# Down products that read the second weight's columns in pairs 64 apart, in an attention and gated-layer kernel

## Chip, cores and metric

The kernel runs on one core of one Trainium2 chip. The metric is the device time of one execution in microseconds (us); the median over several runs is what counts. Engines: TensorE (PE, with its weight loads as PEld), VectorE (DVE), ScalarE (ACT), GpSimd (POOL) and SyncE (SP, which issues the DMAs here).

## The reference

Two stages. The first is a linear attention with a decaying state, for 4 batches, 8 heads, 768 tokens and heads of 48:

```python
for t in range(S):
    state = alpha[:, :, t, :, None] * state + einsum('bhd,bhe->bhde', k[:, :, t], v[:, :, t])
    y[:, :, t] = einsum('bhd,bhde->bhe', q[:, :, t], state)
```

The second takes the 3072 tokens of 384 numbers through a gated layer of 2048:

```python
h = x @ w_in                      # (3072, 384) @ (384, 2048)
sp = where(h > 20, h, log1p(exp(minimum(h, 20))))
g = h * tanh(sp)
return (g @ w_out).astype(float32)   # (3072, 2048) @ (2048, 384)
```

The weights arrive as 64-bit numbers; the result is float32.

## The kernel before

Tokens are handled in 24 chunks of 128 rows (two batches of 64 tokens each, C = 128). Attention is done chunk by chunk; its result x stands in SBUF as `xs`, transposed and split into an upper and a lower float32r part. Each weight is likewise split into two float32r parts, `wi` (w_in) and `wo` (w_out, `[128, 2, 16, 384]`), as it arrives: VectorE takes the 64-bit words apart (lines 435 to 445) and makes most of the remainders (line 464), ScalarE rounds (line 450). Later the weights are loaded again and checked on ScalarE (lines 502 and 505).

The gated layer is cut into units: one of the 16 slices f of the 2048 inner columns, for two chunks (the first segments) or four (the others). The list SEGMENTS says in which order. A unit does:

- the up products, line 819: 9 matmuls (3 blocks of rows by 3 pairs of upper and lower parts). The stationary tile is a block of `wi`, the moving one is `xs` through `by_token`, which takes a chunk's 128 columns as pairs: column t of the first batch, then column t of the second, 64 words further on. For four chunks that is 512 columns;
- the gate: five ScalarE operations (lines 828 to 846) and two of VectorE (840, 849), which leave `g`, again in two parts, columns in the order of the pairs;
- the down products, line 877: for each chunk 3 matmuls, the stationary tile a 128x128 block of `g`, the moving one `wo[:, z, f]`, 384 columns in their order. They add up over f in one PSUM bank per chunk.

Four banks o0 to o3 hold these sums. When a segment leaves its chunks before the last f, the sums are stashed in SBUF by ScalarE (`stash`, line 897). At the last f a stashed part is added by VectorE (`join`, line 904), and `result` (line 911) is a ScalarE copy with a running sum for a final test, from PSUM where nothing was stashed, from SBUF after a join. Then SP stores the rows (line 918).

The order of the work is made by a planner in the kernel's own code, class Plan. Each step is a task with an engine, a cost and a lateness (table COST, in us) and a key; keys are moved by hand-kept numbers (SHIFT), the banks of early attention chunks are listed (EARLY_BANKS). `order` walks through time and takes, over all engines, the task that can begin first, keys breaking ties; buffers go round in the order of keys. Where TensorE would be idle before 130 planned us, it puts in filling matmuls (line 928) on bf16 zeros-and-ones data of 384 columns, whose result nobody reads. The order found is written into the program; on the chip each engine keeps to it and waits by semaphores.

The lines that matter:

```python
by_token = lambda t: t.rearrange("p n (x t) -> p n t x", x=2)
# line 819
p[:, :N], wi[:, z, s, fs], by_token(x[:, s, :, a]), start=m == 0,
# line 877
o.tile[:, :DM], g.tile[:, a, j * C : (j + 1) * C], wo[:, z, f],
```

Of the kernel before, what the change touches and what calls it, by code (L numbers as in the profile page):

```python
# [14 lines left out]
AF = mybir.ActivationFunctionType  # L15
# [14 lines left out]
P = 128  # L30
# [37 lines left out]
FILL_FROM, FILL_UNTIL = 2.0, 130.0  # L68
FILL_MARGIN = 0.1
EARLY_BANKS = {  # L70
    0: "att o0 o1 att h".split(),
    1: "att att h o2 h".split(),
    2: "o2 o1 att o0 att".split(),
    3: "att o0 o3 att att".split(),
    4: "att att o2".split(),
    5: "att o2 att".split(),
    10: "o1 o2 o3".split(),
    11: "att o1 att".split(),
    12: "o1 o2 o0".split(),
    13: "att o3 att".split(),  # L80
    14: "att o2 o0".split(),
    15: "h att att".split(),
    16: "o0 o1 att".split(),
    17: "o1 att o3".split(),
    18: "o0 o1 att".split(),
    19: "att att h".split(),
    20: "att o2 att".split(),
    21: "att o0 h".split(),
    23: "att h att".split(),
}  # L90
SHIFT = {
    "chunk": {
# [4 lines left out]
    },  # L97
    "unit": {
# [16 lines left out]
    },  # L115
    "weight": {
        0: -6.4516, 1: -18.694, 2: -0.0718, 3: -5.3782, 4: 0.59055, 5: -3.1028, 6: 0.22915,
        7: 3.6276, 8: -0.93908, 9: 4.1863, 10: -1.3406, 11: -0.89088, 12: 0.60959, 13: 2.7395,
        14: 2.9243, 15: 3.4437,
    },  # L120
    "weight check": {
        0: 3.4663, 1: 0.17532, 3: 5.129, 4: 4.2064, 5: 0.81532, 6: 4.6598, 7: 4.2295, 8: -5.8016,
        9: 1.9332, 10: -0.19251, 11: -6.9069, 12: -0.12023, 13: -4.9148, 14: 4.4556, 15: 14.881,
    },
}
X_PE = 4
# [25 lines left out]
class Plan:  # L152
# [131 lines left out]


WINDOW = 10**6
SAME = 0.2
QUEUE = 8
DMA_FIRST, DMA_LAST = 1.67, 0.3
SLACK, SLACK_FROM = (0.5, 0.3), 12.0  # L290

COST = {
    "load part": (0.47, 0.9), "load qk": (0.47, 1.75), "load q": (0.47, 3.2),
    "load v": (0.47, 0.6), "load w": (0.45, 2.35), "move": (0.625, 0.15), "store": (0.62, 0.9),
    "cold fill": (0.321, 0.36), "fill": (0.1635, 0.2), "off": (0.21, 0.37), "w off": (0.965, 1.09), "lead": (0.27, 0.37), "bits": (0.47, 0.585), "w hi": (0.415, 0.53), "w lo": (0.95, 1.08),
    "w check": (0.89, 1.1),
    "scan": (1.152, 1.27), "inverse": (0.113, 0.21), "mult k": (0.562, 0.745), "mult": (0.602, 0.725), "half mult": (0.32, 0.46), "check": (0.2, 0.34),
    "state": (0.272, 0.4), "state0": (0.21, 0.35), "decay": (0.469, 0.605), "mask": (0.335, 0.49),
    "scores0": (0.7, 0.83), "scores": (0.92, 1.06), "y0": (1.15, 1.27), "y": (1.37, 1.5),
    "y last": (0.935, 1.05), "turn": (0.35, 0.68),  # L300
    "turned": (0.415, 0.57), "update": (0.65, 0.87),
    "x hi": (0.265, 0.415), "x lo": (0.333, 0.45),
    "down": (0.5235, 0.79), "stash": (0.36, 0.5), "join": (0.468, 0.59), "result": (0.485, 0.61),
}
for _n in range(1, 5):
    _c = 128 * _n
    COST["up", _n] = (9 * (0.428e-3 * _c + 0.01), 9 * (0.428e-3 * _c + 0.01) + 0.205)
    COST["exp", _n] = (0.142 + 0.836e-3 * _c, 0.29 + 0.836e-3 * _c)
    COST["act", _n] = (0.094 + 0.836e-3 * _c, 0.237 + 0.836e-3 * _c)
    COST["ln", _n] = (0.186 + 0.836e-3 * _c, 0.327 + 0.836e-3 * _c)  # L310
    COST["dve", _n] = (0.069 + 1.045e-3 * _c, 0.21 + 1.045e-3 * _c)
# [4 lines left out]
def fast_path(ctx, tc, qka, v, w, out, good):  # L316
# [28 lines left out]
    minus1 = const.tile([P, 1], F32, name="minus1")  # L345
    nc.vector.memset(minus1, -1.0)
    by_pair = lambda t: t.rearrange("p (j t) -> p j t", j=NPAIR)
    by_token = lambda t: t.rearrange("p n (x t) -> p n t x", x=2)
    by_half = lambda t: t.rearrange("p (j x t) -> p j x t", j=NPAIR, x=2)
    by_seg = lambda t: t.rearrange("p (n t) -> p n t", n=NSEG)  # L350
# [28 lines left out]
    def new(buffer, shape, name, pool=None, dtype=F32):  # L379
        buffer.tile = (pool or sb).tile(  # L380
            shape, dtype, tag=buffer.tag, name=name, bufs=plan.slots[buffer.tag]
        )
        return buffer.tile
# [421 lines left out]
    def unit(c0, nt, f, at, ends):  # L805
# [61 lines left out]
        for j in range(nt):  # L867
            n = c0 + j
            begins = n not in sums
            if begins:  # L870
                sums[n] = bank(f"o{BANK[n]}")
            o, end = sums[n], ends(n)

            def down(o=o, j=j, n=n, begins=begins, end=end):
                within(o)
                for m, (a, z) in enumerate(((0, 0), (0, 1), (1, 0))):
                    made = nc.tensor.matmul(  # L877
                        o.tile[:, :DM], g.tile[:, a, j * C : (j + 1) * C], wo[:, z, f],
                        start=begins and m == 0, stop=end and m == 2,
                    )  # L880
                if f == NFF - 2 and j == 0:
                    late[mybir.EngineType.PE] = made

            t_down = add(
                "PE", *COST["down"], key + LAG + 0.001 * j, down, [t_lo, *ready_w[f, 1]], [g, o],
                behind=downs.get(n, []),
            )
            downs[n] = [t_down]
            if not end:
                continue  # L890
            del sums[n]
            k = key + LAG + 0.1
            if f < NFF - 1:
                part[n] = plan.buffer("osb")

                def stash(o=o, n=n):
                    nc.scalar.copy(new(part[n], [P, DM], f"part{n}"), o.tile[:, :DM])

                kept[n] = add("ACT", *COST["stash"], k, stash, [t_down], [o, part[n]])
                continue  # L900
            done, from_part = [t_down], n in kept
            if from_part:
                def join(o=o, n=n):
                    nc.vector.tensor_tensor(part[n].tile, o.tile[:, :DM], part[n].tile, ALU.add)

                done = [add("DVE", *COST["join"], k, join, [t_down, kept[n]], [o, part[n]])]
            osb = part[n] if from_part else plan.buffer("osb")

            def result(o=o, n=n, osb=osb, from_part=from_part):
                to = osb.tile if from_part else new(osb, [P, DM], f"osb{n}")  # L910
                nc.scalar.activation(
                    to, to if from_part else o.tile[:, :DM], AF.Copy, accum_out=ochk[:, n : n + 1]
                )

            def store(n=n, osb=osb):
                b, c = chunks[n]
                to = out[2 * b * S : 2 * (b + 1) * S, :].rearrange("(x s) d -> s x d", x=2)
                nc.sync.dma_start(to[c * HALF : (c + 1) * HALF], osb.tile)

            written = add("ACT", *COST["result"], k, result, done, [osb] if from_part else [o, osb])  # L920
            add("SP", *COST["store"], k, store, [written], [osb])

# [274 lines left out]
```

## Time and profile before

| what | value |
|---|---|
| median of 3 runs | 500.67 us (500.38 to 500.82) |
| the profiled execution | 500.14 us |
| its span, first to last instruction | 498.3 us |
| mean granted TensorE clock | 0.997 |
| TensorE matmuls busy | 481.0 us, 5229 of them |
| ScalarE busy | 396.8 us |
| VectorE busy | 326.0 us |
| moved by DMA | 56.82 MB |

All times are of one profiled execution, in us from the first instruction, unless ns is written. Matmuls overlap: one starts while the one before is still ending, so the mean time of one is longer than the distance between two, and a busy TensorE need not be at its peak. "Idle before" is an engine's idle time in front of the instructions of a row, with what ended it. The chain is the work that ended last, followed back from the end; a piece of it on TensorE holds a run of matmuls, with their count. A line such as L877 is a line of the kernel before.

### The profile page before, as it was taken

Reading aid. Unit: us, or ns where it says so; the run is one execution under the profiler, and the core shown is the slowest. Engines: PE = TensorE matmul, PEld = TensorE weight load, DVE = VectorE, ACT = ScalarE, POOL = GpSimd, SP = SyncE. Lnnn points to the kernel's source line nnn. Section 1 sums busy time; section 2 is a strip of 40 time slices with the busy share of each in tenths; the row PEclk is TensorE's granted clock in tenths of the full one; section 3 lists DMA queues with packets and bytes.
Section 4 is the critical chain, followed back from the end, with each engine's and each line's share of the span. In section 5 each row is a group of like instructions: output and inputs, shape, how many; then the busy total and the mean of one; then the engine's idle time right before and its main releaser. Section 6 shows DMA issues by size and latency. Waiting matters only on the chain.

```text
span 498.3 us, 12735 instructions
## 1 busy us (share of the span) xinstructions
PE 481.0 (97%) x5229; PEld 431.9 (87%) x5229; DVE 326.0 (65%) x632; ACT 396.8 (80%) x902; POOL 2.4 (0%) x12
## 2 busy tenths in 40 slices
PE   7999999999999999999999999999999999999994
PEld 4578989989888989879988899999889899999993
DVE  8999999999994777788623489633383433333231
ACT  2677988998989997989998866866966868877872
POOL 1000000000000000000000000000000000000000
PEclk9999999999999999999999999999999999999998
DMA  8686435433334735675330254000130000100001
GB/s 304 213 289 218 155 126 195 149 111 143 128 128 135 270 116 197 215 265 180 144 122 0 75 172 142 32 1 1 64 99 17 8 11 0 53 11 2 0 1 68
DMA packets 20079, 56.82 MB, mean 114 GB/s; under 512 B 4016, under 2 KB 12464, under 8 KB 20016
## 3 DMA queue, kind: packets, MB, share of 16 engines
q1 hardware_dynamic: 20016, 55.96, 32.2%
q8 instruction: 42, 0.69, 0.5%
q14 instruction: 21, 0.17, 0.1%
HBM read 48.87 MB, written 4.72 MB: 108 GB/s over the span
## 4 chain that ended last, share of the span: by engine, by line
PE 55%; DVE 20%; ACT 19%; issue 4%; DMA 1%; ACTq 0%; DVEq 0%
PE bank L877 24%; PE bank L819 21%; PE bank L608 4%; ACT t L834 3%; DVE t L840 3%; ACT t L828 3%; DVE g L849 2%; DVE w_lead L445 2%; DVE w_lead L440 2%; ACT t L831 2%; ACT wc L502 2%; ACT g L846 2%; ACT wc L505 2%; ACT t L837 2%; DVE rest L562 2%
## 5 line engine op out<-in xcount | busy, mean ns | idle before, releaser
L877 PE MATMUL bank<-wo,g 128*128 128x384 f32 x1152 | 218.4, 339 | 1.1 <-DVE xs L691 1.1
L819 PE MATMUL bank<-xs,wi 128*128 128x512 f32 (+1 forms) x954 | 206.1, 364 | 2.8 <-DVE t L840 2.4
L877 PEld LDWEIGHTS bank<-wo,g 128*128 128x128 f32 x1152 | 202.0, 188 | 6.3 <-issue 1.7
L819 PEld LDWEIGHTS bank<-xs,wi 128*128 128x128 f32 x954 | 165.1, 189 | 25.7 <-DVE t L840 6.9
L840 DVE SCALAR_TENSOR_TENSOR t<-t,bank 128x512 f32<-128x512 f32 (+1 forms) x106 | 67.7, 638 | 96.7 <-ACT t L837 96.6
L849 DVE SCALAR_TENSOR_TENSOR g<-t,g 128x512 fp32r<-128x512 f32 (+1 forms) x106 | 67.2, 643 | 40.6 <-ACT g L846 40.4
L846 ACT ACTIVATE g<-t 128x512 fp32r<-128x512 f32 (+1 forms) x106 | 61.0, 584 | 29.4 <-PE bank L877 18.1
L828 ACT ACTIVATE t<-bank 128x512 f32<-128x512 f32 (+1 forms) x106 | 58.1, 549 | 29.7 <-PE bank L819 25.6
L834 ACT ACTIVATE t<-t,fifth 128x512 f32<-128x512 f32 (+1 forms) x106 | 71.9, 679 | 1.7
L837 ACT ACTIVATE t<-t 128x512 f32<-128x512 f32 (+1 forms) x106 | 62.2, 588 | 1.6
L831 ACT ACTIVATE t<-t 128x512 f32<-128x512 f32 (+1 forms) x106 | 62.1, 587 | 1.5
L562 DVE TENSOR_TENSOR_SCAN rest<-qka,behind 112x520 f32<-112x520 f32 x24 | 29.8, 1242 | 0.4 <-DMA qka<-in_qka_dram 0.3
L575 DVE TENSOR_TENSOR_SCAN qka<-qka,ahead 112x520 f32<-112x520 f32 x24 | 29.7, 1236 | 0.0
L686 ACT ACTIVATE xs<-bank 112x256 fp32r<-112x256 f32 x48 | 16.0, 382 | 10.2 <-PE bank L672 6.4
L642 DVE COPY_PREDICATED probs<-causal,bank 128x256 f32<-128x256 uint32 x48 | 18.7, 440 | 3.7 <-PE bank L631 3.7
L608 PE MATMUL bank<-qka,state 48*48 48x64 f32 (+1 forms) x704 | 20.2, 221 | 0.7 <-ACT t L831 0.4
L828 ACT ACTIVATION_READ_ACCUMULATOR t<-bank 128x1 f32 x106 | 20.6, 195 | 0.0
L792 DVE TENSOR_TENSOR state<-bank,state 112x192 f32<-112x192 f32 x40 | 13.2, 353 | 9.7 <-PE bank L672 5.7
L608 PEld LDWEIGHTS bank<-qka,state 48*48 48x48 f32 (+1 forms) x704 | 15.7, 127 | 4.3 <-issue 2.1
L445 DVE SCALAR_TENSOR_TENSOR w_lead<-ws,w_lead 128x384 int32<-128x384 int32 x32 | 19.3, 605 | 0.0
L440 DVE SCALAR_TENSOR_TENSOR w_lead<-ws,w_lead 128x384 int32<-128x384 int32 x32 | 19.0, 608 | 0.0
L608 PEld LDWEIGHTS bank<-probs,v 64*48 64x48 f32 (+1 forms) x768 | 13.4, 127 | 6.3 <-issue 2.1
(76 smaller groups left out, 343.0 us busy)
## 6 DMA issues: line engine op xcount, KB each, us to landing
qka<-in_qka_dram SPq DMA_DIRECT2D x22, 772.5 KB, 5.4
ws<-in_wp_dram SPq DMA_DIRECT2D x16, 768.0 KB, 4.1
wc<-in_wp_dram SPq DMA_DIRECT2D x16, 768.0 KB, 5.1
v<-in_vp_dram SPq DMA_DIRECT2D x24, 192.0 KB, 3.0
out_dram<-osb SPq DMA_DIRECT2D x16, 192.0 KB, 2.3
xs<-xs SPq DMA_DIRECT2D x144, 16.0 KB, 3.2
out_dram<-part SPq DMA_DIRECT2D x8, 192.0 KB, 2.3
qka<-in_qka_dram SPq DMA_DIRECT2D x2, 260.5 KB, 3.6
```

What stands on the lines that cost most here:

```text
L562: nc.vector.tensor_tensor_scan(t[:, :0:-1], alpha()[:, :0:-1], behind[:, ::-1], 0.0, ALU.mult, ALU.max)
L575: nc.vector.tensor_tensor_scan(a, a, ahead, 0.0, ALU.mult, ALU.max)
L608: return nc.tensor.matmul(summed(x)[HALF * side : HALF * side + wide, j], weights(wide), moving, start=start, stop=stop, skip_group_check= ...
L819: nc.tensor.matmul(p[:, :N], wi[:, z, s, fs], by_token(x[:, s, :, a]), start=m == 0, stop=m == len(passes) - 1,)
L828: nc.scalar.activation(wide(t), wide(h), AF.Exp, accum_out=uchk[:, at : at + 1])
L831: nc.scalar.activation(wide(t), wide(t), AF.Square, bias=1.0)
L834: nc.scalar.activation(wide(t), wide(t), AF.Ln, bias=fifth, scale=0.2)
L837: nc.scalar.activation(wide(t), wide(t), AF.Exp, scale=-1.0)
L840: nc.vector.scalar_tensor_tensor(wide(t), wide(t), 2.5, wide(h), ALU.subtract, ALU.mult)
L846: nc.scalar.activation(g.tile[:, 0, :N], wide(t), AF.Copy, scale=-0.4)
L849: late[mybir.EngineType.DVE] = nc.vector.scalar_tensor_tensor(g.tile[:, 1, :N], wide(t), -0.4, g.tile[:, 0, :N].bitcast(F32), ALU.mult, AL ...
L877: made = nc.tensor.matmul(o.tile[:, :DM], g.tile[:, a, j * C : (j + 1) * C], wo[:, z, f], start=begins and m == 0, stop=end and m == 2,)
```

## The change

The down products read the 384 columns of `wo[:, z, f]` through `spread`: in each block of 128 columns, column t and column t + 64 follow each other. The PSUM bank so holds the columns in that order. `stash`, `join` and `result` read the bank through `in_order` (every second word, then the others) and write SBUF in the columns' order, so the stores are unchanged. The planner's tables are new: costs, shifts, banks of the early chunks, and SAME.

```diff
@@ tables
-    0: "att o0 o1 att h".split(),
+    0: "o3 att att o0 o1".split(),
...
-SAME = 0.2
+SAME = 0.155
...
-    "load q": (0.47, 3.2), "store": (0.62, 0.9), "w off": (0.965, 1.09),
+    "load q": (0.47, 3.0), "store": (0.62, 0.7), "w off": (0.925, 1.07),
-    "scores0": (0.7, 0.83), "scores": (0.92, 1.06), "y0": (1.15, 1.27), "y": (1.37, 1.5),
+    "scores0": (0.68, 0.81), "scores": (0.88, 1.02), "y0": (1.1, 1.22), "y": (1.32, 1.45),
-    "down": (0.5235, 0.79),
+    "down": (0.495, 0.75),
-    COST["up", _n] = (9 * (0.428e-3 * _c + 0.01), 9 * (0.428e-3 * _c + 0.01) + 0.205)
+    COST["up", _n] = (9 * (0.4075e-3 * _c + 0.008), 9 * (0.4075e-3 * _c + 0.008) + 0.195)
@@ fast_path
+    spread = lambda t: t.rearrange("p (n x t) -> p n t x", n=NK, x=2)
+    in_order = lambda t: t.rearrange("p (n t x) -> p n x t", n=NK, x=2)
+    as_rows = lambda t: t.rearrange("p (n x t) -> p n x t", n=NK, x=2)
@@ down
-                        o.tile[:, :DM], g.tile[:, a, j * C : (j + 1) * C], wo[:, z, f],
+                        o.tile[:, :DM], g.tile[:, a, j * C : (j + 1) * C], spread(wo[:, z, f]),
@@ stash
-                    nc.scalar.copy(new(part[n], [P, DM], f"part{n}"), o.tile[:, :DM])
+                    to = as_rows(new(part[n], [P, DM], f"part{n}"))
+                    nc.scalar.copy(to, in_order(o.tile[:, :DM]))
@@ join
-                    nc.vector.tensor_tensor(part[n].tile, o.tile[:, :DM], part[n].tile, ALU.add)
+                    to = as_rows(part[n].tile)
+                    nc.vector.tensor_tensor(to, in_order(o.tile[:, :DM]), to, ALU.add)
@@ result
-                    to, to if from_part else o.tile[:, :DM], AF.Copy, accum_out=ochk[:, n : n + 1]
+                    as_rows(to), as_rows(to) if from_part else in_order(o.tile[:, :DM]), AF.Copy,
+                    accum_out=ochk[:, n : n + 1],
```

## Rows read from the trace of the kernel before

**Rows 1.** The page: busy us, share and count of each engine; shares of the chain.

```profile
PE 481.0 (97%) x5229; PEld 431.9 (87%) x5229; DVE 326.0 (65%) x632; ACT 396.8 (80%) x902; POOL 2.4 (0%) x12
...
PE 55%; DVE 20%; ACT 19%; issue 4%; DMA 1%; ACTq 0%; DVEq 0%
```

**Rows 2.** Busy time by stage: stage, its length, engines (instructions), PEclk, DMA share, GB/s.

```profile
0.00:50.00 50.00, 45.24 (x811) 33.03 (x812) 46.33 (x100) 28.89 (x83) 2.43 (x12) 1.00 0.72 256
50.00:150.00 100.00, 97.80 (x977) 89.29 (x976) 97.20 (x206) 88.62 (x220) 0.00 (x0) 1.00 0.41 141
150.00:275.00 125.00, 122.57 (x1450) 110.62 (x1449) 81.08 (x145) 116.32 (x259) 0.00 (x0) 1.00 0.47 164
275.00:492.00 217.00, 215.24 (x1997) 198.95 (x1995) 101.23 (x182) 163.00 (x344) 0.00 (x0) 1.00 0.12 41
492.00:498.30 6.30, 0.13 (x2) 0.02 (x2) 0.15 (x1) 0.00 (x0) 0.00 (x0) 0.75 0.29 102
```

**Rows 3.** TensorE by line and shape: count, busy us, mean ns, idle before.

```profile
L877 PE MATMUL bank<-wo,g 128*128 128x384 f32 x1152 | 218.4, 339 | 1.1 <-DVE xs L691 1.1
...
L928 PE MATMUL bank<-behind 112*128 112x384 bf16 x63 | 13.9, 362 | 2.4 <-DVE behind L355 2.4
```

**Rows 4.** The chain in order of time: start us, us, runs of up and down products.

```profile
56.42 1.04 PE bank L819 x9
...
186.68 7.34 PE bank L877 x42
...
336.86 6.29 PE bank L877 x36
...
437.94 3.88 PE bank L819 x18
441.83 4.24 PE bank L877 x24
```

**Rows 5.** The order of time, TensorE, two groups of filling products: start us, us, count.

```profile
13.40 1.15 PE L928 MATMUL bank<-behind 112*128 112x384 bf16 x6
...
19.33 2.29 PE L928 MATMUL bank<-behind 112*128 112x384 bf16 x13
```

**Rows 6.** Busy time by stage of line 877 alone: stage, length, PE, PEld, PEclk, DMA.

```profile
0.00:50.00 50.00, 4.48 (x21) 3.46 (x22) 1.00 0.72 256
50.00:150.00 100.00, 47.59 (x245) 42.30 (x243) 1.00 0.41 141
150.00:275.00 125.00, 55.18 (x293) 51.53 (x294) 1.00 0.47 164
275.00:492.00 217.00, 111.17 (x597) 104.71 (x595) 1.00 0.12 41
```

**Rows 7.** ScalarE and VectorE by line and shape: count, busy us, mean ns, idle before.

```profile
L831 ACT ACTIVATE t<-t 128x512 f32<-128x512 f32 x86 | 53.9, 627 | 1.2
...
L502 ACT ACTIVATE wc<-wc 128x768 f32<-128x768 f32 x16 | 16.8, 1052 | 1.9 <-DMA wc<-in_wp_dram 1.9
...
L435 DVE TENSOR_SCALAR w_lead<-ws 128x384 int32<-128x384 int32 x32 | 11.7, 388 | 0.1
...
L831 ACT ACTIVATE t<-t 128x256 f32<-128x256 f32 x20 | 8.2, 418 | 0.3
...
L911 ACT ACTIVATE osb<-bank 128x384 f32<-128x384 f32 x16 | 7.8, 488 | 2.0 <-PE bank L877 2.0
...
L904 DVE TENSOR_TENSOR part<-bank,part 128x384 f32<-128x384 f32 x8 | 4.2, 554 | 3.1 <-PE bank L877 3.1
...
L897 ACT COPY part<-bank 128x384 f32<-128x384 f32 x8 | 3.7, 480 | 0.0
```

**Rows 8.** The order of time at the end, ScalarE's last result.

```profile
491.10 0.49 ACT L911 ACTIVATE osb<-bank 128x384 f32<-128x384 f32 x1
```

More of the change, by code (lines that the diff above doesn't have):

```diff
@@ L70 @@
 EARLY_BANKS = {
-    0: "att o0 o1 att h".split(),
[L72 to L89, printed above, removed]
+    0: "o3 att att o0 o1".split(),
+    1: "att att o1 o2 att".split(),
+    2: "att att o0 o2 h".split(),
+    3: "att att att o3 o0".split(),
+    4: "h att att".split(),
+    5: "o2 att att".split(),
+    10: "att att o0".split(),
+    11: "o3 o2 att".split(),
+    12: "att o0 att".split(),
+    13: "o0 o3 o1".split(),
+    14: "o3 att att".split(),
+    16: "att att o0".split(),
+    17: "o2 att o3".split(),
+    18: "att o1 o2".split(),
+    20: "att o1 o0".split(),
+    21: "att att o3".split(),
+    22: "att o0 att".split(),
 }
@@ L92 @@
     "chunk": {
[4 rows of a table removed]
[4 rows of a table added]
     },
     "unit": {
[16 rows of a table removed]
[15 rows of a table added]
     },
     "weight": {
-        0: -6.4516, 1: -18.694, 2: -0.0718, 3: -5.3782, 4: 0.59055, 5: -3.1028, 6: 0.22915,
-        7: 3.6276, 8: -0.93908, 9: 4.1863, 10: -1.3406, 11: -0.89088, 12: 0.60959, 13: 2.7395,
-        14: 2.9243, 15: 3.4437,
+        0: -1.3645, 1: -3.9266, 2: -1.9803, 3: -84.561, 4: 3.3556, 6: 0.12802, 7: -0.8727,
+        8: 4.997, 9: -1.2263, 10: -0.63618, 11: -1.2721, 12: 16.098, 13: 13.353, 14: 20.447,
+        15: 23.272,
     },
     "weight check": {
-        0: 3.4663, 1: 0.17532, 3: 5.129, 4: 4.2064, 5: 0.81532, 6: 4.6598, 7: 4.2295, 8: -5.8016,
-        9: 1.9332, 10: -0.19251, 11: -6.9069, 12: -0.12023, 13: -4.9148, 14: 4.4556, 15: 14.881,
+        0: -5.1754, 1: -0.0025102, 2: 1.7889, 3: -4.3521, 4: 3.9291, 5: -3.2842, 6: 0.18132,
+        7: -1.7127, 8: 2.4011, 9: -12.335, 10: -4.6595, 11: 12.393, 12: 2.9451, 13: -3.1735,
+        14: -4.3042, 15: -0.022134,
     },
@@ L292 @@
 COST = {
-    "load part": (0.47, 0.9), "load qk": (0.47, 1.75), "load q": (0.47, 3.2),
-    "load v": (0.47, 0.6), "load w": (0.45, 2.35), "move": (0.625, 0.15), "store": (0.62, 0.9),
-    "cold fill": (0.321, 0.36), "fill": (0.1635, 0.2), "off": (0.21, 0.37), "w off": (0.965, 1.09), "lead": (0.27, 0.37), "bits": (0.47, 0.585), "w hi": (0.415, 0.53), "w lo": (0.95, 1.08),
+    "load part": (0.47, 0.9), "load qk": (0.47, 1.75), "load q": (0.47, 3.0),
+    "load v": (0.47, 0.6), "load w": (0.45, 2.35), "move": (0.625, 0.15), "store": (0.62, 0.7),
+    "cold fill": (0.32, 0.36), "fill": (0.1635, 0.2), "off": (0.21, 0.37), "w off": (0.925, 1.07), "lead": (0.27, 0.37), "bits": (0.47, 0.585), "w hi": (0.415, 0.53), "w lo": (0.95, 1.08),
     "w check": (0.89, 1.1),
@@ L298 @@
     "state": (0.272, 0.4), "state0": (0.21, 0.35), "decay": (0.469, 0.605), "mask": (0.335, 0.49),
-    "scores0": (0.7, 0.83), "scores": (0.92, 1.06), "y0": (1.15, 1.27), "y": (1.37, 1.5),
-    "y last": (0.935, 1.05), "turn": (0.35, 0.68),
+    "scores0": (0.68, 0.81), "scores": (0.88, 1.02), "y0": (1.1, 1.22), "y": (1.32, 1.45),
+    "y last": (0.88, 0.99), "turn": (0.34, 0.66),
     "turned": (0.415, 0.57), "update": (0.65, 0.87),
     "x hi": (0.265, 0.415), "x lo": (0.333, 0.45),
-    "down": (0.5235, 0.79), "stash": (0.36, 0.5), "join": (0.468, 0.59), "result": (0.485, 0.61),
+    "down": (0.495, 0.75), "stash": (0.36, 0.5), "join": (0.468, 0.59), "result": (0.485, 0.61),
 }
```

39 rows, old and new, of the table SHIFT are left out of this document.

## The prediction

> **What bounds the kernel now.** I read the page's busy totals first, for an engine that could set the end. TensorE's products are busy 481.0 of 498.3 us, ScalarE 396.8, VectorE 326.0 [rows 1]. The table of busy time by stage comes next, because such an average mixes stages [rows 2]. From 275 to 492 us products fill 215.24 of 217 us while ScalarE has 54 us free and VectorE 116: there only a shorter product brings the end nearer. From 50 to 275 us TensorE is as full, but VectorE (97.20 of 100 us, 50 to 150) and then ScalarE (116.32 of 125 us, 150 to 275) are nearly full too: there a shorter product may only wait longer. In the first 50 us TensorE is partly kept busy by 63 filling products without use [rows 3].
>
> "Busy" says nothing of pace, since products overlap: a down product lasts 339 ns in the rows [rows 3]. The pace is seen in the chain of waits, where a run of products stands with its length and its count [rows 4]. Three long runs of down products take 7.34, 6.29 and 4.24 us for 42, 36 and 24: 17.87 us for 102, **175.2 ns for 384 columns**, 0.456 ns a column. A run of 18 up products takes 3.88 us, **215.6 ns for 512 columns**, 0.421 ns a column. The clock granted is 1.00 in every stage to 492 us, the 2.4 GHz level [rows 2], so both are rates at one clock. The filling products have the down products' width, 384: a group of 13 takes 2.29 us and one of 6 takes 1.15, so 7 more take 1.14 us, **163 ns each** [rows 5]. So of three kinds of product only the down products are slow, by 12 ns each.
>
> What sets them apart? A matmul's own fixed share does not: narrow up products, with a weight load of the same 128x128 before each, come every 116 ns (1.04 us for 9) [rows 4], so neither the load nor the issue holds a product to 175. The clock does not. The filling products read 384 neighbouring two-byte words. Up and down both read four-byte words, and the code differs in their order: line 819 takes them in pairs 64 words apart (by_token), line 877 takes 384 neighbours. The fast four-byte stream is the one in pairs. That is what the change gives the down products.
>
> **The change, part by part.**
>
> *The moving operand of the down products (line 877).* Nothing is added; 1152 products [rows 3] read the same words in another order. Paces of before that bound it: 161.7 ns (the up products' 215.6 / 512 x 384) and 175.2 ns (no gain). I take 163 ns, the row of the same width; the up products, in the same order of reading, lie nearest to it. 1152 x (175.2 - 163) = **14.1 us**; with 161.7 it would be 15.6. By stage the counts are 21, 245, 293 and 597 (groups on an edge are counted twice) [rows 6], so about 0.3, 3.0, 3.6 and 7.3 us.
>
> *Sums put in order when taken out.* The PSUM tile now holds the columns paired; 16 results (line 911) and 8 stashes (line 897) on ScalarE and 8 joins (line 904) on VectorE read it at every second word, and write neighbours. No instruction is added. The other 8 results read SBUF in order as before. No row shows a PSUM read at every second word. The nearest rows read SBUF so: line 502 squares 768 such words in 1052 ns, where the straight line through 512 and 256 neighbouring words (627 and 418 ns) gives 836, so 0.28 ns a word more, 0.108 us for 384; VectorE's line 435 reads 384 such words in 388 ns, about one ns a word [rows 7]. Bounds: 0 and 32 x 0.108 = 3.5 us of engine time. All but the last four results lie beside products; what covers them is a group of down products on another bank, and without that cover a unit that begins on the bank would wait 0.1 us a time. The last four stand on the end: the last begins at 491.10 us [rows 8], and the closing test in the code needs it. So 0 to 0.4 us; I take **+0.2**.
>
> *Given back to ScalarE and VectorE.* What is saved before 275 us, 3.0 + 3.6 + 0.3 = 6.9 us, can turn into waits where those engines are full [rows 2]. Part of their work there has no date: the planner takes weight splits on VectorE and weight checks on ScalarE whenever they can begin first, and the stage after 275 us has room for them. Bounds 0 and 6.9; I take **+1.5**, nearer to 0 because TensorE itself is 98% busy in both stages.
>
> *The new order.* Costs, shifts and banks of the planner change; loads, stores, splits, checks and attention are moved on all queues (SP's loads and row moves with them), but none is added or dropped. The old table gave a four-chunk group of up products 2.06 us, the chain shows 1.94 [rows 4], the new table has 1.95. What an order can win: TensorE is unbusy 17.3 us [rows 1], 6.2 of them the end, 2.4 the wait before the first product [rows 2, 3], so 8.7 in between, and the fillers' 13.9 us hide more waiting. What it can lose: as much again, 8.7 us. I choose **-2 us**, a quarter of the 8.7, since the new table lies nearer to the paces above; this is the weakest term. Work delayed by the new order would show as idle time of TensorE in front of up products, for x or for a free bank.
>
> **The sum** stands on the profiled execution: 500.14 us, of which the span is 498.3 and 1.84 lies around it. 500.14 - 14.1 + 0.2 + 1.5 - 2.0 = 485.7. The median of the runs is 0.53 above the profiled one, so **486.3 us**.
>
> **The rivals.** *The pace stays (0.10).* The down products could be slow for another reason than their order of reading: their stationary tile g is written by two engines shortly before, and they go round four banks. Against it: inside runs of 36 and 42 the pace is even, and a bank is kept for three products at a time. Then only the new order counts: 500.67 less 2, give or take 6, about 495 to 505.
>
> *The gain is swallowed before 275 us (0.05).* If ScalarE and VectorE truly set the pace from 50 to 275 us, only 7.3 us is left, and nothing comes from the order: 500.67 - 7.3 + 0.4 = 493.8. For it: VectorE and ScalarE hold 20% and 19% of the chain [rows 1], and the stage is full [rows 2]. Against it: TensorE's 98%.
>
> *Reading apart costs more (0.05, slower).* Place: the moving read of line 877. Neighbours in the stream are 256 bytes apart, and no near word is read twice in a row. Price by the nearest such read, line 502: 1052 against 836, 26% more [rows 7]. At 26% a down product takes 220.8 ns, 45.6 ns more, 1152 times: 52.5 us, some 553 us. It decides as soon as the pace passes 177 ns, where the 2 us of the order are used up. Against it stand the up products, which read so at 0.421 ns a column [rows 4]. The Trainium skill has this as a rule: "Advanced Engine Details and Errata", section SBUF Cachelines, says that reads are at full rate when they hit one 16-byte line again, and that a different line for each access costs a penalty; by it the change would be a loss. This trace disagrees for TensorE's moving operand: the stream that never stays on a line is the fastest per column.
>
> **How the numbers follow.** The forecast (pace near 163, most of it kept) has 0.80. Low end: 15.6 us from the pace and 5.6 from the order, 500.67 - 21.2 = 479.5. High end: only the stage after 275 us counts, 493.8, so 494. That holds nearly all of the forecast's cases and about half of the second rival's; the other two lie outside. A measurement of this kernel tells 0.2%, 1.0 us, from no change. Faster: 0.80 + 0.05 + 0.04 of the first rival = 0.89; same 0.03, from the first rival; slower 0.03 of it + 0.05 = 0.08.
>
> **What would show it.** Right: runs of down products in the chain at 161 to 165 ns each, up products still at 215 to 216, results and stashes at 480 to 600 ns, TensorE's unbusy time between start and end below 10 us. Wrong: down products still at 175; or at 163 with new idle time in front of up products between 50 and 275 us; or line 911 far over 0.6 us with TensorE waiting for a bank behind it. A time under 479 would mean that the order, not the pace, did much of it.

## The result, and the profile after

The changed kernel takes **485.65 us** (median of 4 runs, 484.02 to 486.19) against 500.52 for the kernel before beside it: a ratio of 0.9697, interval 0.9673 to 0.9721. The forecast was 486.3, faster. The total came true; two of its parts did not, as the experiments show.

Lines are those of each run's own kernel: the up and down products are L820 and L878 in the kernel after and L822 and L880 where the pairs are put into the kernel before.

The page of the kernel after: busy us, share and count of each engine, and the shares of the chain of waits, to be set against [rows 1].

```profile
PE 469.4 (97%) x5246; PEld 419.1 (87%) x5246; DVE 327.6 (68%) x632; ACT 395.2 (82%) x902; POOL 2.4 (1%) x12
...
PE 55%; DVE 19%; ACT 17%; DMA 5%; issue 3%; SPq 1%; ACTq 0%; DVEq 0%
```

TensorE is busy 11.6 us less, and still holds only 55% of the chain. The groups by line and shape (count, busy us, mean ns, idle before), against [rows 3, 7]:

```profile
L878 PE MATMUL bank<-wo,g 128*128 128x384 f32 x1152 | 206.1, 329 | 0.2
...
L820 PE MATMUL bank<-xs,wi 128*128 128x512 f32 x774 | 183.0, 383 | 2.4 <-DVE t L841 2.3
...
L932 PE MATMUL bank<-behind 112*128 112x384 bf16 x80 | 17.7, 357 | 2.4 <-DVE behind L356 2.4
...
L914 ACT ACTIVATE osb<-bank 128x384 f32<-128x384 f32 x16 | 7.7, 490 | 1.7 <-PE bank L878 1.7
...
L907 DVE TENSOR_TENSOR part<-bank,part 128x384 f32<-128x384 f32 x8 | 4.1, 549 | 0.0
L899 ACT COPY part<-bank 128x384 f32<-128x384 f32 x8 | 3.6, 480 | 0.0
```

Results, joins and stashes, which now read PSUM at every second word, last 490, 549 and 480 ns; before they lasted 488, 554 and 480. There are 80 filling products instead of 63: more TensorE time early without work. Two runs of products in the chain (start us, us, count), against [rows 4]:

```profile
290.92 3.88 PE bank L820 x18
294.80 3.90 PE bank L878 x24
```

Up products stand at 3.88 / 18 = 215.6 ns, as before. Down products have gone from 175.2 to 3.90 / 24 = **162.5 ns**. Over 1152 products that is 14.6 us, and the kernel is 14.9 us faster. It looks as if nothing more need be asked.

### The profile page after: what moved, and what is told of

It is laid out like the page before. It is cut to its first block, busy times and chain, and to the rows that moved or that the text cites. A ratio compares the mean times of both kernels' runs of the same rounds, so it can differ in the third digit from the quotient of the medians.

```text
span 482.3 us, 12792 instructions
## 1 busy us (share of the span) xinstructions
PE 469.4 (97%) x5246; PEld 419.1 (87%) x5246; DVE 327.6 (68%) x632; ACT 395.2 (82%) x902; POOL 2.4 (1%) x12
## 4 chain that ended last, share of the span: by engine, by line
PE 55%; DVE 19%; ACT 17%; DMA 5%; issue 3%; SPq 1%; ACTq 0%; DVEq 0%
PE bank L820 24%; PE bank L878 23%; PE bank L609 4%; DMA wc<-in_wp_dram 3%; DVE w_lead L446 3%; DVE w_lead L441 3%; ACT wc L506 2%; DVE t L841 2%; DVE g L850 2%; ACT t L835 2%; ACT t L829 2%; ACT g L847 2%; ACT t L838 2%; ACT wc L503 2%; ACT t L832 2%
## 5 line engine op out<-in xcount | busy, mean ns | idle before, releaser
L820 PE MATMUL bank<-xs,wi 128*128 128x512 f32 (+1 forms) x954 | 207.2, 364 | 2.4 <-DVE t L841 2.3
L878 PE MATMUL bank<-wo,g 128*128 128x384 f32 x1152 | 206.1, 329 | 0.2
L878 PEld LDWEIGHTS bank<-wo,g 128*128 128x128 f32 x1152 | 189.2, 189 | 6.0 <-DVE g L850 1.0
L820 PEld LDWEIGHTS bank<-xs,wi 128*128 128x128 f32 x954 | 164.4, 189 | 24.4 <-DVE t L841 6.0
L609 PEld LDWEIGHTS bank<-probs,v 64*64 64x64 f32 (+1 forms) x768 | 13.5, 127 | 7.5 <-issue 2.8
L932 PE MATMUL bank<-behind 112*128 112x384 bf16 x80 | 17.7, 357 | 2.4 <-DVE behind L356 2.4
L506 ACT ACTIVATE wc<-wc 128x768 f32<-128x768 f32 x16 | 19.0, 1189 | 0.0
```

The lines of the kernel that those rows point to most:

```text
L609: return nc.tensor.matmul(summed(x)[HALF * side : HALF * side + wide, j], weights(wide), moving, start=start, stop=stop, skip_group_check= ...
L820: nc.tensor.matmul(p[:, :N], wi[:, z, s, fs], by_token(x[:, s, :, a]), start=m == 0, stop=m == len(passes) - 1,)
L878: made = nc.tensor.matmul(o.tile[:, :DM], g.tile[:, a, j * C : (j + 1) * C], spread(wo[:, z, f]), start=begins and m == 0, stop=end and m ...
```

## The experiments

Two theories for the 14.9 us. One: the shorter products gave it. The other: the new order of work gave it, and the shorter products mostly wait. For each run below its time is a ratio to the kernel before on the same chip; "us gained" is (1 - ratio) x 500.5.

### The pairs alone, and the new order alone

On the kernel before, with its own tables:

```diff
-    o.tile[:, :DM], g.tile[:, a, j * C : (j + 1) * C], wo[:, z, f],
+    o.tile[:, :DM], g.tile[:, a, j * C : (j + 1) * C], spread(wo[:, z, f]),
```

(with stash, join and result as in the change).

> The kernel before with the pairs 64 apart alone: its tables and its order of work stay. Theory (the order of reading sets the pace): down products every 162 to 164 ns, up products still every 215 to 216, and 1152 x 12.5 ns = 14.4 us less, at most 2 us given back where ScalarE and VectorE are full: 486 to 489 us. Rival (the new order of work made a good part of the gain): 490 to 495 us. Rival (the pace belongs to g or to the banks): down products still every 175 ns, 500 us.

Measured: 498.11 us, ratio 0.9968 (0.9953 to 0.9984). **1.6 us** gained instead of 12 to 14: outside the ranges of the theory and of both rivals.

On the kernel after, the reverse edit, with the three steps that take sums out as they were:

```diff
-    o.tile[:, :DM], g.tile[:, a, j * C : (j + 1) * C], spread(wo[:, z, f]),
+    o.tile[:, :DM], g.tile[:, a, j * C : (j + 1) * C], wo[:, z, f],
```

> The kernel after with its new tables and order, but the down products read 384 neighbouring words again, and the sums are taken out as they stand. Theory: down products every 175 ns again and nearly all of the gain gone: 498 to 501 us. Rival (the new order of work carries a part): 490 to 496 us with the same 175 ns, less waiting of TensorE.

Measured: 489.70 us, ratio 0.9787 (0.9774 to 0.9800), **10.7 us** gained with the slow products. So the rival of this run holds, just past the fast end of its range: of 15.2 us (0.9697), the order alone gives 10.7, the pairs on top of it 4.5, the pairs alone 1.6.

The profile says why. First the pairs in the old order: shares of the chain, and two runs of products in it.

```profile
PE 45%; ACT 25%; DVE 20%; DMA 4%; issue 4%; SPq 1%; ACTq 0%; DVEq 0%
```

```profile
339.65 5.85 PE bank L880 x36
...
452.89 3.90 PE bank L880 x24
```

The products are as short as they can be, 162.5 ns, but TensorE's share of the chain has fallen from 55% [rows 1] to 45%: what was saved has become waiting. Then neighbours in the new order, chain shares and one run:

```profile
PE 94%; DMA 3%; DVE 2%; issue 0%; ACT 0%; SPq 0%
```

```profile
306.85 4.20 PE bank L878 x24
```

Products at 175.0 ns, and TensorE holds 94% of the chain, from start to end. Yet give this order the short products (the kernel after), and the share falls back to 55%: VectorE and ScalarE stood close behind. The busy time of all engines by stage shows how near (stage, its length, then PE, PEld, DVE, ACT and POOL with counts, then PEclk, DMA share, GB/s):

```profile
50.00:160.00 110.00, 109.96 (x1107) 102.34 (x1100) 103.06 (x217) 98.68 (x249) 0.00 (x0) 1.00 0.39 132
160.00:290.00 130.00, 130.00 (x1736) 119.23 (x1736) 89.47 (x166) 122.00 (x278) 0.00 (x0) 1.00 0.52 177
```

VectorE is busy 94% of the first stage, ScalarE 94% of the second.

Where the limit lies can be counted. Busy time of the down products alone by stage (stage, its length, PE and count, PEld and count, PEclk, DMA share, GB/s). The kernel before:

```profile
0.00:160.00 160.00, 56.97 (x288) 49.90 (x288) 1.00 0.51 178
160.00:290.00 130.00, 55.14 (x294) 51.64 (x294) 1.00 0.45 159
```

The pairs in the old order:

```profile
0.00:160.00 160.00, 52.81 (x282) 46.06 (x282) 1.00 0.50 175
160.00:290.00 130.00, 51.81 (x294) 48.38 (x294) 1.00 0.44 156
```

Neighbours in the new order:

```profile
0.00:160.00 160.00, 56.49 (x289) 50.35 (x290) 1.00 0.49 171
160.00:290.00 130.00, 59.63 (x312) 53.98 (x311) 1.00 0.52 177
```

The kernel after:

```profile
0.00:160.00 160.00, 52.87 (x289) 47.07 (x289) 1.00 0.49 169
160.00:290.00 130.00, 55.66 (x308) 50.30 (x309) 1.00 0.53 179
```

By 290 us the kernel before has done 582 down products and the one with short products in the same order 576; in the new order it is 601 with slow products and 597 with short ones. In either order, products that are 7% shorter bring none of them forward in the first 290 us. Behind that some 550 to 576 are left, 7 us at 12.7 ns each, and that alone shows in the time, less what was lost before.

Counts at one instant are rough; the start of one and the same product is not. The traces give, for the 300th, the 600th and the last of the 1152 down products, in us:

| kernel | 300th | 600th | last |
|---|---|---|---|
| before | 167.5 | 296.9 | 490.7 |
| pairs in the old order | 169.7 | 300.5 | 488.4 |
| neighbours in the new order | 164.1 | 289.5 | 481.7 |
| after | 164.2 | 290.6 | 476.5 |

With short products the 600th begins 3.6 us *later* in the old order and 1.1 us later in the new one. Engines that are only full could hold TensorE to its old pace, but that alone would not put it behind. Something grew slower as well. ScalarE's weight checks and VectorE's steps that take the 64-bit words apart read every second word of SBUF (the checks write there too). Their rows before, one of the steps and the two checks of a weight (count, busy us, mean ns):

```profile
L445 DVE SCALAR_TENSOR_TENSOR w_lead<-ws,w_lead 128x384 int32<-128x384 int32 x32 | 19.3, 605 | 0.0
...
L505 ACT ACTIVATE wc<-wc 128x768 f32<-128x768 f32 x16 | 17.3, 1084 | 0.0
...
L502 ACT ACTIVATE wc<-wc 128x768 f32<-128x768 f32 x16 | 16.8, 1052 | 1.9 <-DMA wc<-in_wp_dram 1.9
```

The same three with the pairs in the old order:

```profile
L448 DVE SCALAR_TENSOR_TENSOR w_lead<-ws,w_lead 128x384 int32<-128x384 int32 x32 | 20.8, 652 | 0.0
...
L508 ACT ACTIVATE wc<-wc 128x768 f32<-128x768 f32 x16 | 19.5, 1219 | 0.0
...
L505 ACT ACTIVATE wc<-wc 128x768 f32<-128x768 f32 x16 | 18.5, 1156 | 2.0 <-DMA wc<-in_wp_dram 2.0
```

In the new order they go from 585, 1016 and 1038 ns with neighbours to 617, 1189 and 1132 with pairs. Over all checks and all three steps, ScalarE has 3.8 us more to do in the old order and 4.3 in the new one, VectorE 4.3 and 2.9.

What slows them is the order in which TensorE reads beside them. The next table sorts the checks, and VectorE's second and third steps, by the products that TensorE was running for over 90% of their time: mean ns, with the count. Its last row is a run of a later section, in which the up products read neighbours.

| kernel | up, down products read | check beside up | check beside down | step beside up | step beside down |
|---|---|---|---|---|---|
| before | pairs, neighbours | 1278 (7) | 897 (5) | 678 (13) | 588 (15) |
| pairs in the old order | pairs, pairs | 1275 (9) | 1226 (6) | 692 (13) | 690 (16) |
| neighbours in the new order | pairs, neighbours | 1257 (4) | 904 (9) | 660 (11) | 559 (22) |
| after | pairs, pairs | 1276 (4) | 1235 (8) | 664 (12) | 661 (16) |
| after, up products' neighbours | neighbours, pairs | 890 (4) | 1269 (5) | 553 (15) | 630 (14) |

A check beside pairs takes 1142 to 1325 ns, beside neighbours 886 to 942: the two do not overlap, and whichever product reads neighbours has the fast checks beside it. ScalarE's gate steps (L831), which read 512 words in order, take 626 ns beside up products and 627 beside down products before. In the order of time, a check beside up products and one beside down products, before:

```profile
214.02 2.21 PE L819 MATMUL bank<-xs,wi 128*128 128x512 f32 x9 [0.55 <-DVE t L840]
...
214.59 1.28 ACT L502 ACTIVATE wc<-wc 128x768 f32<-128x768 f32 x1
...
216.07 1.21 PE L877 MATMUL bank<-wo,g 128*128 128x384 f32 x6
216.34 0.89 ACT L505 ACTIVATE wc<-wc 128x768 f32<-128x768 f32 x1
```

So the change made the two full engines slower as well, by 8.1 us of work in the old order and 7.2 in the new one. That is enough for the 3.6 and 1.1 us by which TensorE falls behind, but no run takes the slowing away by itself. How the lost gain divides, between engines that were full anyway and engines that grew slower, is not shown: the runs of the next section make the slowed steps short, and so lift both at once.

### Relieving the other two engines

If ScalarE and VectorE hold the first 290 us, making their work lighter without touching the order must bring the short products' gain out:

```diff
-    nc.scalar.activation(high(), high(), AF.Square, accum_out=wchk[:, 0, f : f + 1])
+    nc.scalar.activation(high()[:, :16], high()[:, :16], AF.Square, accum_out=wchk[:, 0, f : f + 1])
...
-    high(), high(), AF.Exp, scale=-(2.0**32), accum_out=wchk[:, 1, f : f + 1]
+    high()[:, :16], high()[:, :16], AF.Exp, scale=-(2.0**32), accum_out=wchk[:, 1, f : f + 1]
...
-    lead.tile, words(0), 29, lead.tile, ALU.logical_shift_right, ALU.bitwise_or
+    lead.tile[:, :16], words(0)[:, :16], 29, lead.tile[:, :16], ALU.logical_shift_right, ALU.bitwise_or
```

Both, on the kernel after:

> The kernel after in its order, with both other engines relieved by the same instructions on fewer columns: the weight checks (two ScalarE operations for each of 16 weights) look at 16 of 768 words, and the third step of taking the words apart on VectorE (32 operations) sets the lowest three bits in 16 of 384 columns only, so the checks are partial and the weights a little rounded. Theory (up to some 300 us VectorE, then ScalarE, sets the pace once the down products are fast, and that hid most of the gain): 474 to 479 us, 7 to 11 us under the kernel after. Rival (the order, the banks or TensorE itself hold it): 484 to 486 us.

Both, on the new order with neighbours:

> The same relief, in the new order with neighbours (the second run of this study). Its chain of waits is TensorE's from start to end, so theory: nearly no gain, 487 to 490 us; the distance to the run with relief and pairs is then 11 to 14 us, near the 1152 x 12.5 = 14.4 us of the pace, where without relief it was 4. Rival (both kernels gain alike from the relief): 480 us, and the distance stays 4.

The first two edits alone (ScalarE), on the kernel after:

> The kernel after with ScalarE's weight checks on 16 of 768 words alone; VectorE's work is whole. Theory (VectorE is the limit from 50 to 160 us, ScalarE from 160 to 300): the time lost against the full pace comes back behind 160 us only: 3 to 6 us under the kernel after, 480 to 483 us. Rival (VectorE alone holds it): 485 to 486.

The third alone (VectorE), on the kernel after:

> The kernel after with VectorE's third step on 16 of 384 columns alone; the checks are whole. Theory: TensorE gets some 2 to 3 us ahead by 160 us and loses it again where ScalarE is full: 483 to 486 us. Rival (VectorE alone holds it): 474 to 479.

Measured:

| kernel | us | ratio (interval) | us gained |
|---|---|---|---|
| after | 485.65 | 0.9697 (0.9673 to 0.9721) | 15.2 |
| both relieved, pairs | 475.70 | 0.9491 (0.9475 to 0.9507) | 25.5 |
| new order, neighbours | 489.70 | 0.9787 (0.9774 to 0.9800) | 10.7 |
| both relieved, neighbours | 488.41 | 0.9748 (0.9730 to 0.9765) | 12.6 |
| ScalarE relieved, pairs | 480.21 | 0.9580 (0.9564 to 0.9596) | 21.0 |
| VectorE relieved, pairs | 480.90 | 0.9599 (0.9579 to 0.9618) | 20.1 |

The relief is worth 10.3 us with short products and 1.9 with slow ones. The distance between pairs and neighbours grows from 4.5 to **12.9 us**, close to the 14.4 of the pace. So the theory holds, and the rival (both gain alike) falls. Each engine alone gives about half, 5.8 and 4.9, and the two add up. The last run came out better than its expectation (483 to 486): VectorE's lead is not lost again to ScalarE, as the starts of single products below show.

Relieved, with neighbours, the same two stages read so (engines as before):

```profile
50.00:160.00 110.00, 109.72 (x1097) 102.44 (x1096) 95.71 (x219) 96.13 (x249) 0.00 (x0) 1.00 0.40 137
160.00:290.00 130.00, 130.00 (x1736) 119.15 (x1736) 89.64 (x166) 101.44 (x274) 0.00 (x0) 1.00 0.51 174
```

VectorE is now busy 87% of the first and ScalarE 78% of the second; this is room that the short products can use.

The chain shows each limit go. Relieved of both, with pairs:

```profile
PE 95%; DVE 1%; DMA 1%; ACT 1%; issue 0%; SPq 0%
```

ScalarE relieved:

```profile
PE 84%; DVE 11%; DMA 2%; ACT 1%; issue 1%; SPq 1%; DVEq 0%
```

VectorE relieved:

```profile
PE 74%; ACT 18%; DMA 3%; issue 3%; DVE 2%; SPq 0%; ACTq 0%; DVEq 0%
```

and the down products by stage show where. ScalarE relieved:

```profile
0.00:160.00 160.00, 53.56 (x291) 47.47 (x291) 1.00 0.49 170
160.00:290.00 130.00, 56.07 (x315) 51.52 (x315) 1.00 0.52 180
```

VectorE relieved:

```profile
0.00:160.00 160.00, 55.31 (x303) 49.57 (x304) 1.00 0.52 180
160.00:290.00 130.00, 54.18 (x301) 48.84 (x300) 1.00 0.49 167
```

With VectorE lighter, 303 products are begun by 160 us instead of 289; with ScalarE lighter, the first stage stays at 291 and the second has 315 instead of 308. (Counts at one instant are rough, as up products may just be running.) The starts of the same products, in us, say it more exactly:

| kernel | 300th | 600th | last |
|---|---|---|---|
| after | 164.2 | 290.6 | 476.5 |
| ScalarE relieved | 163.5 | 285.3 | 471.7 |
| VectorE relieved | 159.4 | 285.7 | 472.7 |
| both relieved | 159.5 | 281.6 | 468.1 |

VectorE's relief brings 4.8 us by the 300th product and almost nothing behind it; ScalarE's brings 0.7 by then and 5.3 by the 600th. In the kernel after, **VectorE is the limit to about 160 us, ScalarE from there to 290.**

### The same loss in the up products

On the kernel after, the up products read neighbours:

```diff
-    p[:, :N], wi[:, z, s, fs], by_token(x[:, s, :, a]), start=m == 0,
+    p[:, :N], wi[:, z, s, fs], x[:, s, :, a], start=m == 0,
```

The first form also stored the rows to match, as two halves of 64:

```diff
-    to = out[2 * b * S : 2 * (b + 1) * S, :].rearrange("(x s) d -> s x d", x=2)
-    nc.sync.dma_start(to[c * HALF : (c + 1) * HALF], osb.tile)
+    to = out[2 * b * S : 2 * (b + 1) * S, :].rearrange("(x s) d -> x s d", x=2)
+    nc.sync.dma_start(to[:, c * HALF : (c + 1) * HALF], osb.tile)
```

> The kernel after, with the up products' 512 columns read as neighbours too (64 tokens of one batch, then 64 of the other); the rows of a chunk then stand in that order and are stored in it. Down products stay in pairs. Theory (any stream of neighbouring four-byte words is slow on TensorE): up products go from 215.6 to about 215.6 x 175.2 / 162.6 = 232 ns (256 columns: from 112 to 118 to 120), 774 x 16.7 + 180 x 7 = 14.2 us more: 498 to 501 us. Rival (it was something about wo, g or the sums' banks): up products at 215 to 216 and 485 to 487 us.

Measured: 538.08 us, ratio 1.0758 (1.0741 to 1.0775), a miss by 38 us. The waits name the reason, which is not TensorE (engine and line, waited for: us, times, longest):

```profile
DVE rest L563 <- DMA qka<-in_qka_dram: 34.8, 6, 10.9
...
PE bank L609 <- DMA v<-in_vp_dram: 16.1, 3, 6.2
```

Attention's loads come late; in the kernel after the longest of VectorE's waits for them is 0.4 us. The last four stores now keep SP for 7.81 us in the order of time:

```profile
514.57 7.81 SPq L922 DMA_DIRECT2D out_dram<-osb  x4
```

against 2.49 in the kernel after. SP issues the loads too, and they wait behind such stores. So the run was made again with the stores as they were:

> The up products read neighbours as in the run before of that kind, but the stores stay as they are in the kernel after, so the 128 rows of a chunk are stored in another order of tokens. Theory: up products at 231 ns for 512 columns and 119 to 120 for 256 again, 13.5 us more work for TensorE; up to some 290 us part of it goes into waits that are there anyway, so 490 to 495 us, and no DMA keeps anyone waiting longer than in the kernel after (its 538 us came from the stores in two halves of 64 rows). Rival (reading neighbours costs the up products more than the pace): over 500 us.

Measured: 489.70 us, ratio 0.9786 (0.9757 to 0.9814). Two runs of its chain:

```profile
290.49 4.13 PE bank L820 x18
294.62 3.90 PE bank L878 x24
```

Up products at 4.13 / 18 = 229 ns instead of 215.6, down products untouched: the loss belongs to the order of reading, not to `wo`, `g` or the banks. Again some 12 us more work for TensorE (774 x 13.8 ns and the narrow ones) moved the time by only 4.5 us, just under the range given. Much of it filled waits (TensorE's share of the chain goes from 55% to 88%), and the checks beside the up products took 890 ns instead of 1276. The form of the stores makes the 48 us between the two runs. In the order of time, a check beside up products and one beside down products now, to be set against those of the kernel before:

```profile
218.18 1.78 PE L820 MATMUL bank<-xs,wi 128*128 128x512 f32 x7
...
218.54 0.89 ACT L503 ACTIVATE wc<-wc 128x768 f32<-128x768 f32 x1
...
226.07 2.11 PE L878 MATMUL bank<-wo,g 128*128 128x384 f32 x12
...
226.64 1.29 ACT L506 ACTIVATE wc<-wc 128x768 f32<-128x768 f32 x1
```

### Which orders of reading are fast

Two runs of one execution each, with eight orders each, chosen by the slice f:

```diff
+    read_in = [
+        lambda o, g, w, s, e: nc.tensor.matmul(o, g, w, start=s, stop=e),
+        lambda o, g, w, s, e: nc.tensor.matmul(o, g, w.rearrange("p (n x t) -> p n t x", x=2, t=2), start=s, stop=e),
...
+    ]
...
-    made = nc.tensor.matmul(
+    made = read_in[f % len(read_in)](
```

> The kernel after, with the down products' order of reading chosen by the slice f, eight kinds, each for two of the sixteen f: neighbours; pairs 2, 4, 8, 16, 32 and 64 words apart; every second word. The sums of different f then no longer belong to the same column, so the output's columns are jumbled; all instructions and sizes stay. Theory A (two words in a row from one piece of 16 bytes are slow): neighbours 175 ns, pairs 2 apart slow as well, pairs 4 apart and more 162 to 164, every second word between. Theory B (any two words that are not next to each other are fast): all but neighbours at 162 to 164. Theory C (a longer distance is needed): the pace falls only at 8, 16, 32 or 64. The time as a whole: 485 to 496 us, by how many kinds are slow, 144 x 12.5 ns = 1.8 us for each.

> Eight more orders of reading for the down products, by slice f, two of the sixteen each: neighbours; neighbours backwards; every fourth word; fours 32 apart; pairs 192 apart; sixes 64 apart; two neighbours here and two 192 on; four neighbours here and four 192 on. The output's columns are jumbled again. From the first such run (neighbours 175, pairs 2 apart 174, 4 and more apart 162, every second word 340): theory A1 (two words in a row from one 16-byte piece cost something, two from a piece and then the next piece without change of place cost more): backwards 175 or more, every fourth word 162 to 165 or, if a steady march through pieces is what costs, over 300; all that alternate between places far apart with each word 162 to 163; two and four neighbours here and there 170 to 176. Theory A2 (only the distance to the word before counts): two neighbours here and there about halfway, 169.

Measured, as the median time from the start of a down product of 384 columns to the start of the next product (144 of a kind):

| order of the four-byte words | ns |
|---|---|
| neighbours; the same backwards | 175; 176 |
| pairs 2 apart | 174 |
| pairs 4, 8, 16, 32, 64 and 192 apart | 162 to 163 |
| four neighbours here, four 192 on | 194 |
| fours 32 apart | 204 |
| sixes 64 apart | 231 |
| two neighbours here, two 192 on | 247 |
| every second word; every fourth | 340; 347 |

In the order of time a run of 12 shows it: its length less one product's own time, over 11. From the first run, every second word (L814, a product lasts 0.52 us), pairs 2 apart (L808, 0.34) and pairs 4 apart (L809, 0.33):

```profile
323.11 4.25 PE L814 MATMUL bank<-wo,g 128*128 128x384 f32 x12
...
333.18 2.25 PE L808 MATMUL bank<-wo,g 128*128 128x384 f32 x12
335.27 2.11 PE L809 MATMUL bank<-wo,g 128*128 128x384 f32 x12
```

From the second, every fourth word (L809, 0.53) and fours 32 apart (L810, 0.37):

```profile
353.11 4.32 PE L809 MATMUL bank<-wo,g 128*128 128x384 f32 x12
...
361.15 2.61 PE L810 MATMUL bank<-wo,g 128*128 128x384 f32 x12
```

Theory A of the first run fits its pairs: 4 words, 16 bytes, is enough. It misses every second word, which it put between neighbours and pairs. The second run breaks every simple form of it: fours and sixes never touch a 16-byte piece twice in a row and are slower than neighbours, and two or four neighbours here and there are far from the 169 to 176 of either theory. What is fast, of the orders of four-byte words tried here, is two single words in turn, 16 bytes or more apart, and nothing else. Why is open. The whole times are 505.7 us, over the 485 to 496 expected, and 537.9; one execution each, with the slow kinds in them, they say nothing more.

### Two versions meant to be faster

Since ScalarE's weight checks stand between 145 and 275 us, where it is the limit, they were spread over a longer time:

```diff
+        behind = [started[int(CHECK_BEHIND + f * CHECK_EVERY)]]
-        t = add("SP", *COST["load w"], key - 4, load, uses=[again])
+        t = add("SP", *COST["load w"], key - 4, load, behind, uses=[again])
```

> A version meant to be faster, whole in its work: the kernel after, its tables unchanged, but the planner may load a weight for its check only after the up products of unit 26 + 2.5 f have begun, so the 16 checks (some 34 us of ScalarE) are spread from 160 to 380 us instead of standing from 145 to 275. Theory (ScalarE is a limit from 160 to 290 us, where its relief gave 5.3 us): 2 to 4 us under the kernel after, 481.5 to 484 us. Rival (what is moved back fills the room that TensorE's part after 290 us needs): 485 to 489.

and, with some keys of SHIFT moved as well:

```diff
-    "bits": (0.47, 0.585), "w check": (0.89, 1.1),
+    "bits": (0.55, 0.665), "w check": (1.06, 1.21),
```

> The same idea (checks from unit 25.9 + 2.75 f on), with two costs of the planner set to what the chain showed (a step of taking words apart 0.55 us instead of 0.47, a check 1.06 instead of 0.89) and a handful of SHIFT keys moved to suit. Theory (the planner's order waits because VectorE and ScalarE are costed too low before 290 us): 477 to 482 us. Rival (costs in the table do not matter, the order is bound to differ from its plan): 483 to 488.

Measured: 491.25 us, ratio 0.9809 (0.9785 to 0.9833), for the checks alone, slower than the kernel after, and more than its rival said; 484.44 us, ratio 0.9690 (0.9663 to 0.9717), with the two costs and the keys changed as well, over its theory's 477 to 482, inside its rival's 483 to 488, and not to be told from the kernel after. Between 160 and 290 us ScalarE was less busy in the first of them, 115 of 130 us against 125, and TensorE too, 124 against 128. So room on the engine was not enough; which wait took its place was not followed up. Neither of the two beats the kernel after.

## Why the prediction was right in its total and wrong in its parts

- **The pace of the down products.** Forecast 163 ns, measured 162.5; the reason (pairs against neighbours) held in both directions and for both operands. The first rival, that the pace stays, fell. The third, that reading apart costs more, fell for TensorE: no run of pairs was slower than neighbours. The rule of the Trainium skill behind it ("Advanced Engine Details and Errata", SBUF Cachelines) agrees with every fourth word, a different line each time, which costs twice the time here (347 ns). It does not agree with pairs, also a different line each time (162.5 ns), nor with every second word, two to a line (340 ns).
- **Given back to ScalarE and VectorE: the step that failed.** The prediction read the two full engines before 275 us, priced what could be lost there at 0 to 6.9 us, and took 1.5, "nearer to 0 because TensorE itself is 98% busy in both stages". In the new order 14.6 - 4.5 = 10.1 us was given back, in the old one 13.0. Being 98% busy was no reason: a product lasts 339 ns and the next starts after 175, so a delay of up to 164 ns between two does not show as idle, and the filling products count as busy. What told it was the chain, 55% TensorE's with 20% and 19% for the others [rows 1], and that VectorE was 97% busy in its stage and ScalarE 93% in its own [rows 2]: engines so full have little left to follow a faster one with. The second rival had this mechanism, and 0.05 for it was far too little. Its price of 7.3 us left over was still too high: 1.6 and 4.5 were measured, in good part because by the 600th product TensorE had fallen 3.6 and 1.1 us behind. No term and no rival had what the traces show there: reading in pairs makes ScalarE's checks and VectorE's steps longer. The prediction asked what reading apart costs TensorE, not what it costs the engines beside it. Its own price of such a read, line 502's 1052 ns, was a mean in which the two prices were mixed: over both lines of the checks, 1278 ns beside the pairs of the up products and 897 beside neighbours.
- **The new order: the term that covered it.** Forecast -2 us with bounds of 8.7 either way; measured 10.7 us with slow products and 13.6 (15.2 - 1.6) with short ones, outside the bounds. They were made of TensorE's idle time, which leaves out the same small delays; that these made up the difference is argued, not shown. Which of the tables gives it was not tried: costs, shifts and banks were made for one another.
- **Sums put in order.** Forecast +0.2 with bounds 0 and 3.5 us of engine time; measured nothing: 490 against 488 ns, 549 against 554.
- Two errors, 8.6 us (10.1 given back, not 1.5) and 8.7 us (10.7 from the order, not 2), cancelled, so that the sum came within 0.65 us. That is luck; only the pace and the small term of the sums were rightly read. The prediction named its check, new idle time in front of up products; the page of the kernel after has no more of it (2.4 us on L820, against 2.8 on L819 before). Only the run with one part of the change showed the loss.

## What to carry to other kernels

Before pricing a faster instruction, read stage by stage how full the other engines are: with one of them 93 to 97% busy in a stage, the saving in that stage came to nothing here, whether TensorE held 55% of the chain or 94%; at 78% and 87%, with the slowed steps made short, most of it came, 12.9 of 14.4 us. Then compare the mean times of the *other* engines' steps before and after, also of those that the change does not touch: here the faster read on one engine made reads on two others slower. When a change alters an instruction and the order together, run each part alone: here the order was worth more than the instruction, and 10.7 and 1.6 us alone made 15.2 together. On TensorE, let the moving operand's four-byte words come from two places in turn, 16 bytes or more apart, and look at what reads every second word meanwhile.

## What the runs showed of the hardware that was not expected

The order in which TensorE's moving operand is read changes the time of a product from 162.5 to 347 ns at a granted clock of 1.00, for the same 384 words. While TensorE reads pairs, a ScalarE step on 768 words of SBUF, every second one, takes 1142 to 1325 ns instead of 886 to 942, and VectorE's steps on 384 such words take 630 to 692 ns in the mean instead of 553 to 588; ScalarE's gate steps on neighbouring words do not change (626 and 627 ns). In the run whose loads came late the granted clock had a mean of 0.959: it was 0.90 from 150 to 200 us, a stretch in which TensorE had long waits for loads, so part of its products ran at the lower level, 1.2 GHz. Reading PSUM at every second word cost ScalarE and VectorE nothing (490 against 488 ns, 549 against 554).
